# Expert rows gathered by quarters of channels and turned on VectorE in squares of 32, in an attention and mixture-of-experts kernel

## The chip, the cores and the metric

The kernel runs on one core of one Trainium2 chip. The metric is the device time of one execution in microseconds (us); three executions of the kernel before took 525.34, 525.06 and 520.8 us, median 525.06. The core has five engines with a queue each: TensorE (PE in the profile; its weight loads are PEld), VectorE (DVE), ScalarE (ACT), GpSimd (POOL) and SyncE (SP). [...]

## The reference

The first half is attention with a window and a few global keys; its output, 3072 tokens by 512 channels, is `x`. The second half sends each token to the one expert with the highest cosine score:

```python
logits = xn @ en.T / tau
expert_idx = np.argmax(logits, axis=1)
...
gate_w = probs[np.arange(N), expert_idx]
for e in range(E):                       # E = 8
    mask = expert_idx == e
    h = np.maximum(x[mask] @ w1[e], 0.0)               # 512 -> 1024
    out[mask] = gate_w[mask, None] * (h @ w2[e])       # 1024 -> 512
```

All is float32. The change lies in the second half alone.

## The kernel before, in words

**Attention** takes the first 200 us or so. It writes `x` to memory (`x_dram`, a row of 512 channels a token), chooses each token's expert, and scatters token number and gate into a list of slots by expert (`meta`). A first part of expert 0, 256 tokens, is already begun there.

**The loop over experts** (in the main function, from L1741) then runs eight stages; stage e computes expert e, up to 512 tokens. Each stage has an arm and, from expert 1 on, a pair. The arm (`tc.Switch`, L1384) is compiled for each width of tokens, in steps of 32, and one is chosen at run time; TensorE, ScalarE and VectorE enter it, GpSimd and SyncE don't. In the arm the product with w1 is done by `first_by_seven`: seven products of half-size blocks in place of eight (Strassen's method as Winograd has it), which needs sums of blocks of w1 (`fsum`, made by `first_sums`), and of the tokens (`xsum`, made by `token_sums`, which also overwrites a block of `xT`). Each product is 16 matmuls at L1312, and its result is added by VectorE at L1324 (`plus`); after a `plus` one list of `spare` work is done (`fill`). Behind it come the hidden sums (`hsum`, L1079 to L1082) and the product with w2 for tokens from 256 on (`second_in_arm`, L1245, and `part_in_arm`, L1258).

After the arm, the class `Pair` does the product with w2 for the first 256 tokens, again in seven products (L1117). `Pair.begin` runs the products m, n, n, n; VectorE adds u2 and u3 (L1122) and ScalarE scales them (u2g, u3g). `Pair.end` runs a product into the bank `ps`, which ScalarE reads and scales as p5 (L1170); then `fourth`; then a last product that adds into `ps`, and so has to wait for p5. The rest of the pair, one gated addition y (L1129), is done by VectorE in the next stage, right after its arm. `spare` lists of `Pair.begin` put sums between its additions.

The order on each engine is the order of the program (`manual_schedule`). So what stands ahead of an operation in its engine's queue delays it.

**The rows of the next expert.** `prepare(e + 1)` gathers the token rows with `gather_rows`: four indirect DMAs on GpSimd, each of 128 rows of 2 KB. GpSimd has nothing in the arm or the pair but these gathers and the scatters of results (L1264), so it works ahead: rows for expert e + 2 are gathered while TensorE is in stage e. The buffers `xg` hold eight tiles, two experts' rows. In stage e, `between` calls `turn_row` after some of the products: four TensorE transposes (L1026) of 128x128 into a bank, and two ScalarE copies (L1029) into `xT`, with the tokens laced: 16 by 16 into two halves.

Weights of experts 2 to 7 are loaded by `load_weights` on SyncE, w1 (L167) with channel c x 128 + p on partition p. The load of expert 2's waits for the last scatter of expert 0's results; later ones wait for the first product of the pair before (`out_again`). A `drain` on GpSimd (L1754) stands ahead of each stage.

Of the kernel before, what the change touches and what calls it, by code (L numbers as in the profile page):

```python
# [9 lines left out]
F32 = mybir.dt.float32  # L10
# [10 lines left out]
P = 128  # L21
# [2 lines left out]
PIECES = 32  # L24
FIRST = 256
LACE = 16
WIDTHS = [128] + list(range(160, CAP + 1, 32))
PAIR = WIDTHS.index(256)

# [134 lines left out]

def load_weights(k, e, w):
    nc = k.nc
    first = nc.sync.dma_start(w[0][:], k.w1[e].rearrange("(c p) f -> p c f", p=P))  # L167
    nc.sync.dma_start(w[1][:], k.w2[e].rearrange("(f p) m -> p f m", p=P))
    return first

# [824 lines left out]
def gather_rows(k, ids, xgp, NJ=CAP // P, upto=None):  # L995

    xgs, issued = [], []
    for j in range(NJ):
        xg = xgp.tile([P, k.DM], F32, name="xg", tag="xg")
        i = k.nc.gpsimd.indirect_dma_start(  # L1000
            out=xg[:], out_offset=None, in_=k.x_dram[0 : upto or k.N + 1, :],
            in_offset=bass.IndirectOffsetOnAxis(ap=ids[:, j, 0:1], axis=0),
        )
        xgs.append(xg)
        issued.append(i.ins)
    return xgs, issued


def new_turned(k):
    return k.xtp.tile([P, k.NC, 2, CAP // 2], F32, name="xT", tag="xT")  # L1010

# [280 lines left out]
            between(f)  # L1292


def first_by_seven(k, now, hT, w, between, spare):


    nc, h = k.nc, w // 2
    a = first_weights(k, now.w[0])
    b = [[now.xT[:, 2 * i : 2 * i + 2, j] for j in range(2)] for i in range(2)]  # L1300
    s1, s2, s3, s4 = now.first_sums
    t1, t2, t3, t4 = now.token_sums
    out = [[laced(hT[:, 4 * i : 4 * i + 4, 0:w])[:, j] for j in range(2)] for i in range(2)]
    number = [0]

    def banks():
        return [k.big.tile([P, CAP], F32, name="big", tag="big") for _ in range(2)]

    def product(to, x, y, add=False):
        for f in range(4):  # L1310
            for l in range(2):
                nc.tensor.matmul(to[f // 2][:, f % 2 * 256 : f % 2 * 256 + h], lhsT=x[:, l, f * P : (f + 1) * P], rhs=y[:, l, 0:h],  # L1312
                                 start=not (add or f % 2 or l), stop=True, skip_group_check=True)
        between(number[0])
        number[0] += 1

    def pairs(ps, q):
        for i in range(2):
            x = ps[i][:].rearrange("p (f n) -> p f n", f=2)[:, :, 0:h].rearrange("p f (q i) -> p f q i", i=LACE)
            yield x, q[:, 2 * i : 2 * i + 2]  # L1320

    def plus(ps, z, q, last=False):
        for (x, to), (_, z) in zip(pairs(ps, q), pairs(ps, z)):
            nc.vector.tensor_tensor(out=to, in0=x, in1=z, op=ALU.add)  # L1324
            if last:
                nc.scalar.activation(to, to, AF.Relu)  # L1326
        fill()

    def fill():
        for make in spare.pop(0):  # L1330
            make()

    (q11, q12), (q21, q22) = out
    fill()
    x, y = banks(), banks()
    product(x, a[0][0], b[0][0])
    for ps, q in pairs(x, q21):
        nc.scalar.copy(out=q, in_=ps)
    product(y, s2, t2)
    plus(y, q21, q12)  # L1340
    product(x, a[0][1], b[1][0], True)
    for ps, q in pairs(x, q11):
        nc.scalar.activation(q, ps, AF.Relu)
    product(y, s3, t3, True)
    plus(y, q21, q22)
    v = banks()
    product(v, s1, t1)
    plus(v, q22, q22, True)
    product(y, a[1][1], t4, True)
    plus(y, q21, q21, True)  # L1350
    product(v, s4, b[1][1], True)
    plus(v, q12, q12, True)


def expert(k, now, coming, widths, unfinished):


    tc = k.tc
    w1, w2 = now.w
    hT = new_hidden(k)  # L1360
    if coming:
        coming.xT = new_turned(k)

    def between(f):
        at = {1: (0,), 2: (1,), 3: (2,), 4: (3,)} if now.e else {5: (0,), 6: (1, 2), 7: (3,)}
        for j in at.get(f, ()) if coming else ():
            turn_row(k, coming.rows, coming.xT, j, k.nc.scalar.copy)

    a = [[hT[:, 4 * j : 4 * j + 4, i * P : (i + 1) * P] for j in range(2)] for i in range(2)]
    now.sums, spare = weight_sums(k, w2)  # L1370
    left, making = hidden_sums(k, a)
    more, ahead = [], []
    if coming:
        coming.token_sums, more = token_sums(k, coming.xT)
        if now.e:
            coming.first_sums, ahead = first_sums(k, coming.w[0])
    spare = [spare[:2], spare[2:], ahead[:1], ahead[1:2], more[:2], []]
    if now.e == 1:
        spare[2:6] = [], ahead[:1], ahead[1:2] + more[:1], more[1:2]
    tiles = range(2 if now.e else 1, CAP // P)  # L1380
    ps = None if now.e else k.work0.tile([P, k.DM], F32, name="work", tag="work")
    k.order = list(range(4, 8)) + list(range(4)) if now.e else list(range(8))
    steps = widths_of(now.e)
    for arm in tc.Switch(now.width.index, len(steps), hint=now.width.hint):  # L1384
        w = steps[arm]
        if now.e:
            first_by_seven(k, now, hT, w, between, list(spare))
            for make in making:
                make()
        else:  # L1390
            first_by_eight(k, now.xT, w1, hT, w, between)
        for size in (32, 64):
            if w % (2 * size) >= size:
                part_in_arm(k, now, hT, w2, w // (2 * size) * 2 * size, size)
        for j in tiles:
            if j < w // P:
                second_in_arm(k, now, hT, w2, j)
        if ps:
            second(k, ps, hT, w2, range(k.NF // 2))

    def scatters():
        for j in tiles:
            scatter_rows(k, now.y[:, j - 1, :], now.tile_ids[:, j : j + 1])
        for size in (64, 32):
            scatter_rows(k, now.y_part[size][:], now.parts[size][0], P // size)

    def choose_next():
        if coming:
            give_hint(k, coming.e, widths[coming.e])

    out = [scatters]
    if now.e:
        pair = Pair(k, now.rows, a, left, w2, now.sums, not coming)
        choose_next()
        out += unfinished.pop()()
        number = [lambda: widths.append(take_width(k, now.e + 2))] if now.e + 2 < k.E else []
        if now.e == k.E - 2:
            number.append(lambda: load_flag(k))
        if now.e == 2:
            ahead.append(lambda: flag_leftover(k))  # L1420
        pair.begin(spare=(more[2:], number + ahead[2:3], ahead[3:]))
        ps = k.work0.tile([P, k.DM], F32, name="work", tag="work")
        unfinished.append(pair.end(ps[:, 0:256]))
        out.append(pair.scatter(1))
    else:
        choose_next()
        widths.append(take_width(k, 2))
        out += unfinished.pop()()
        for make in more:
            make()  # L1430
        second(k, ps, hT, w2, range(k.NF // 2, k.NF))
        unfinished.append(lambda: end_second(k, now.rows, ps))
    return out
# [172 lines left out]
def kernel(  # L1606
# [40 lines left out]
    with ExitStack() as moe:  # L1647
# [43 lines left out]
        def prepare(e):  # L1691
            t = Net()
            t.e = e
            t.y, t.y_part = ys[e % 2]
            xgs, t.gathers = gather_rows(n, n.ids[:, e], n.xgp)
            t.rows = n.mt[:, e], n.ids[:, e], xgs
            if e < 2:
                t.w = n.w[e]
            else:
                t.w = new_weights(n, (wp_a, n.wp_b)[e % 2])  # L1700
            return t

        with tc.manual_schedule(engines=ORDERED | set(ARMS) | {mybir.EngineType.Pool}):
# [26 lines left out]
            for j in range(CAP // P):  # L1730
                turn_row(n, coming.rows, coming.xT, j, nc.vector.tensor_copy)
            cast(2, n.E)
            split_rows(n, n.mt)
            for y, parts in ys:
                for x in (y, *parts.values()):
# [5 lines left out]
            for e in range(n.E):  # L1741
                now, coming = coming, None
                parts_of(n, now)
                now.width = widths[e]
                if e == 1:
                    now.first_sums = first
                if e + 1 < n.E:
                    coming = prepare(e + 1)
                for scatter in pending:
                    scatter()  # L1750
                if e and coming:
                    wait_for(n, load_weights(n, e + 1, coming.w), [n.outs[-1] if e == 1 else n.out_again])

                nc.gpsimd.drain()  # L1754
                pending = expert(n, now, coming, widths, unfinished)
# [33 lines left out]
```

## Time and profile before

| | us |
|---|---|
| three executions | 525.34, 525.06, 520.8 |
| the profiled execution, its own time | 523.85 |
| its span in the profile | 522.0 |
| VectorE busy | 301.3 |
| ScalarE busy | 197.4 |
| GpSimd busy | 148.7 |

The stretches of the stages, and how busy TensorE and VectorE are in each, in us:

| stage | from | to | TensorE busy | VectorE busy | DMA share |
|---|---|---|---|---|---|
| 1 | 234.2 | 268.6 | 33.06 | 22.11 | 0.69 |
| 2 | 268.6 | 320.8 | 52.20 | 23.15 | 0.34 |
| 3 | 320.8 | 353.7 | 32.90 | 21.35 | 0.53 |
| 4 | 353.7 | 390.5 | 36.51 | 21.86 | 0.47 |
| 5 | 390.5 | 429.6 | 39.10 | 22.22 | 0.45 |
| 6 | 429.6 | 479.0 | 49.40 | 23.22 | 0.20 |
| 7 | 479.0 | 522.0 | 37.55 | 16.19 | 0.09 |

Stages differ with the number of tokens: 1 and 3 use the arm for 320, 4 for 352, 5 and 7 for 384, 6 for 480, 2 for 512. TensorE's granted clock was 0.994 over the span. In a row of the profile, a line such as L1312 is the line of the kernel that issued the instruction, the two names are output and input, and a releaser is what the engine had waited for. A busy share says little by itself; what counts is which work the chain of waits passes through in each stage.

### The profile page before, as it was taken

The page shows a single profiled execution, that of the slowest core. Times are in us where ns is not written, and L with a number is a line of the kernel's source. Part 1 is how long each engine was busy: PE and PEld are TensorE (multiplying, and loading weights), DVE is VectorE, ACT ScalarE, POOL GpSimd, SP SyncE. Part 2 cuts the span into 40 slices and gives each one's busy share as a digit, 9 for nine tenths or more (in the row PEclk, how much of TensorE's full clock was granted, in tenths as well). Part 3 has the DMA queues.
Part 4 walks back from the last instruction along what each step waited for, and adds up shares of the span by engine and source line. Part 5 has one row for each costly group of instructions (what it writes and reads, how often), then busy time and mean ns, then how long its engine had stood idle before and what let it go on. Part 6 is the DMA issues. An engine that isn't in the chain of part 4 may idle for free.

```text
span 522.0 us, 13698 instructions
## 1 busy us (share of the span) xinstructions
PE 500.9 (96%) x5606; PEld 412.8 (79%) x5606; DVE 301.3 (58%) x602; ACT 197.4 (38%) x493; POOL 148.7 (28%) x169
## 2 busy tenths in 40 slices
PE   8999999999987998899989999999999999999995
PEld 7777787787765687859878659989889789859964
DVE  5646667766774664846745606765646644715531
ACT  4966776777644311303222312412312222302210
POOL 4221121432443326253340024153053050013023
PEclk9999999999998999999999999999999999999999
DMA  8989999998524336818682018457066065001001
GB/s 166 202 174 182 220 238 217 222 232 204 131 69 121 104 62 143 251 46 290 207 287 99 2 50 285 156 198 263 3 217 242 4 224 164 1 15 68 0 22 67
DMA packets 111421, 76.32 MB, mean 146 GB/s; under 512 B 87077, under 2 KB 95269, under 8 KB 111281
## 3 DMA queue, kind: packets, MB, share of 16 engines
q1 hardware_dynamic: 102769, 59.00, 42.6%
q0 software_dynamic: 6912, 15.26, 8.7%
q8 instruction: 63, 1.03, 0.9%
q14 instruction: 77, 0.63, 0.5%
q10 hardware_dynamic: 1600, 0.39, 0.3%
HBM read 61.66 MB, written 17.16 MB: 151 GB/s over the span
## 4 chain that ended last, share of the span: by engine, by line
PE 64%; issue 24%; POOL 5%; DVE 3%; ACT 2%; POOLq 1%; DMA 1%; DVEq 0%
PE big L1312 15%; PE big L1117 8%; PE od L512 7%; PE pa L483 6%; PE pa L458 4%; PE work L1258 3%; PE od L522 3%; PE pa L681 3%; PE work L1117 3%; POOL out_dram L1264 3%; PE work L1245 3%; PE work L1026 2%; PE big L1288 2%; PE pa L585 2%; PE work L1036 1%
## 5 line engine op out<-in xcount | busy, mean ns | idle before, releaser
L496 DVE TENSOR_TENSOR ex<-ex,table 126x768 f32<-126x768 f32 x64 | 60.3, 947 | 41.4 <-ACT ex L489 38.5
L1324 DVE TENSOR_TENSOR hT<-big,hT 128x320 f32<-128x320 f32 (+4 forms) x70 | 39.4, 566 | 49.2 <-PE big L1312 46.8
L1264 POOL DMA_INDIRECT out_dram<-y_arm,tids x17 | 17.0, 1002 | 170.4 <-ACT y_arm L1247 121.3
L489 ACT ACTIVATE ex<-pa 126x384 f32<-126x384 f32 (+1 forms) x128 | 53.7, 476 | 24.0 <-PE pa L483 17.7
L1312 PE MATMUL big<-xT,w1t 128*128 128x160 f32 (+4 forms) x336 | 59.4, 330 | 1.3 <-issue 1.3
L1312 PEld LDWEIGHTS big<-xT,w1t 128*128 128x128 f32 x336 | 54.2, 190 | 4.0 <-issue 2.2
L512 PE MATMUL od<-ex,v 126*64 126x192 f32 (+1 forms) x576 | 46.8, 309 | 0.0
L1000 POOL DMA_INDIRECT xg<-x_dram,idss x32 | 32.3, 1011 | 43.9 <-PE big L1312 21.7
L483 PE MATMUL pa<-qT,kT 64*32 64x128 f32 (+3 forms) x2048 | 40.8, 268 | 2.8 <-issue 2.5
L483 PEld LDWEIGHTS pa<-qT,kT 64*32 64x32 f32 (+1 forms) x2048 | 30.5, 107 | 15.2 <-issue 10.6
L512 PEld LDWEIGHTS od<-ex,v 126*64 126x64 f32 x576 | 35.2, 138 | 7.7 <-issue 3.5
L259 POOL DMA_INDIRECT meta<-mt,slot x24 | 27.4, 1141 | 43.8 <-DVE rd L556 17.8
L1312 PE MATMUL big<-xsum,fsum 128*128 128x160 f32 (+4 forms) x224 | 39.6, 330 | 0.0
L1029 ACT COPY xT<-work 128x256 f32<-128x256 f32 x56 | 18.0, 377 | 56.7 <-PE work L1026 55.3
L1312 PEld LDWEIGHTS big<-xsum,fsum 128*128 128x128 f32 x224 | 36.1, 190 | 1.1
L1245 PE MATMUL work<-w2t,hT 128*128 128x512 f32 x80 | 35.1, 593 | 0.0
L1117 PE MATMUL big<-wsum,hsum 128*128 128x256 f32 x136 | 31.1, 380 | 1.5 <-issue 1.0
L1326 ACT ACTIVATE hT<-hT 128x320 f32<-128x320 f32 (+4 forms) x42 | 21.6, 533 | 25.5 <-DVE hT L1324 25.3
L433 POOL COPY v<-v 30x896 f32<-30x896 f32 (+1 forms) x15 | 16.6, 1119 | 49.0 <-DMA v<-in_v_dram 30.5
L1117 PEld LDWEIGHTS big<-wsum,hsum 128*128 128x128 f32 x136 | 25.7, 190 | 6.0 <-issue 1.8
L1245 PEld LDWEIGHTS work<-w2t,hT 128*128 128x128 f32 x80 | 15.1, 190 | 17.7 <-issue 17.6
L1122 DVE TENSOR_TENSOR ptmp<-big,ptmp 128x256 f32<-128x256 f32 x16 | 6.7, 421 | 37.6 <-PE big L1117 16.9
(246 smaller groups left out, 903.0 us busy)
## 6 DMA issues: line engine op xcount, KB each, us to landing
w1t<-in_moe_w_dram SPq DMA_DIRECT2D x6, 2048.0 KB
w2t<-in_moe_w_dram SPq DMA_DIRECT2D x6, 2048.0 KB
v<-in_v_dram SPq DMA_DIRECT2D x32, 192.0 KB
x_dram<-xs SPq DMA_DIRECT2D x23, 256.0 KB
k<-in_k_dram SPq DMA_DIRECT2D x28, 192.0 KB
q<-in_q_dram SPq DMA_DIRECT2D x28, 192.0 KB
w1t<-in_moe_w_dram SPq DMA_DIRECT2D x32, 128.0 KB
w2t<-in_moe_w_dram SPq DMA_DIRECT2D x32, 128.0 KB
```

The costliest lines, as they stand in the source:

```text
L259: i = nc.gpsimd.indirect_dma_start(out=k.meta[:], out_offset=bass.IndirectOffsetOnAxis(ap=slot[:, t : t + 1], axis=0), in_=mt[:, t, :], in ...
L483: i = nc.tensor.matmul(u.sp[e][k0:k1, a * n + c0 : a * n + c1], lhsT=t.kT[rows, j, k0:k1], rhs=t.qT[rows, j * BLK + c0 : j * BLK + c1], st ...
L489: nc.scalar.activation(u.ex[:, e], u.sp[e][0:ROWS, 0 : 2 * u.n].rearrange("p (a c) -> p a c", a=2), AF.Exp, scale=k.scale)
L496: nc.vector.tensor_tensor(out=exv, in0=exv, in1=tab[:, :, 0 : u.n // BLK, :], op=ALU.mult)
L512: nc.tensor.matmul(g.od[a][e * D : (e + 1) * D, at : at + c1 - c0], lhsT=g.v[0:ROWS, 2 * a + e, u.j, :], rhs=u.ex[:, e, a, c0:c1], start=f ...
L1000: i = k.nc.gpsimd.indirect_dma_start(out=xg[:], out_offset=None, in_=k.x_dram[0 : upto or k.N + 1, :], in_offset=bass.IndirectOffsetOnAxis ...
L1117: i = self.k.nc.tensor.matmul(ps, lhsT=x[:, f, :], rhs=w[:, f, :], start=f == 0 and not add, stop=True, skip_group_check=True)
L1245: nc.tensor.matmul(ps[:], lhsT=hT[:, f, j * P : (j + 1) * P], rhs=w2[:, f, :], start=i == 0, stop=i == k.NF - 1)
L1264: i = k.nc.gpsimd.indirect_dma_start(out=k.out.rearrange("t (i m) -> (t i) m", i=n), out_offset=bass.IndirectOffsetOnAxis(ap=ids, axis=0), ...
L1312: nc.tensor.matmul(to[f // 2][:, f % 2 * 256 : f % 2 * 256 + h], lhsT=x[:, l, f * P : (f + 1) * P], rhs=y[:, l, 0:h], start=not (add or f ...
L1324: nc.vector.tensor_tensor(out=to, in0=x, in1=z, op=ALU.add)
L1326: nc.scalar.activation(to, to, AF.Relu)
```

## The change

For experts 2 to 7, rows are no longer turned by TensorE.

- `square_rows` makes a list of row numbers once: `x_dram` is seen as 4 rows of 128 channels a token, and each gather takes, for 32 tokens, their four quarters of channels onto the four groups of 32 partitions.
- `gather_quarters` issues 16 gathers of 128 quarter rows (512 B) an expert, in place of 4 of whole rows. For expert 2, ten stand ahead of the scatters of expert 0's results and six behind them.
- `turn_squares` turns one tile of 128 tokens with one VectorE transpose of 32x32 squares from `xg` straight to `xT`, reading every fourth word. Partition p of `xT` then holds channels 4p to 4p + 3.
- `load_weights` loads w1 of experts 2 to 7 to match: four neighbouring rows a partition.
- The turns stand after the arm, behind the rest of the former pair and ahead of the pair's first addition. All four token sums come after that first addition; two of them stood in the arm before. In the arm, the sums of w2 (`wsum`) move from ahead of the first addition to behind it, and the sums of w1 (`fsum`) to the last two places; the third and fourth sum of w1 both come at the end of `Pair.begin`.

Experts 0 and 1 keep their gathers and their transposes.

```diff
 def load_weights(k, e, w):
-    first = nc.sync.dma_start(w[0][:], k.w1[e].rearrange("(c p) f -> p c f", p=P))
+    first = nc.sync.dma_start(w[0][:], k.w1[e].rearrange("(p c) f -> p c f", p=P))
...
+def square_rows(k):
+    k.squares = k.tp.tile([P, k.E, CAP // P, 4], I32, name="squares")
+    for b in range(4):
+        for g in range(4):
+            k.nc.vector.tensor_scalar(out=k.squares[b * SQ : (b + 1) * SQ, 2:, :, g], in0=k.mt[g * SQ : (g + 1) * SQ, 2:, :, 0],
+                                      scalar1=4.0, scalar2=float(b), op0=ALU.mult, op1=ALU.add)
+
+def gather_quarters(k, ids, xgs, lo, hi):
+    src = k.x_dram[:, :].rearrange("t (b c) -> (t b) c", b=4)
+    for i in range(lo, hi):
+        j, g = divmod(i, 4)
+        k.nc.gpsimd.indirect_dma_start(
+            out=xgs[j][:, g * P : (g + 1) * P], out_offset=None, in_=src,
+            in_offset=bass.IndirectOffsetOnAxis(ap=ids[:, j, g : g + 1], axis=0),
+        )
+
+def turn_squares(k, xgs, xT, j):
+    half = P // 2
+    k.nc.vector.transpose(
+        out=xT[:, :, :, j * half : (j + 1) * half].rearrange("p c a (g i) -> p g c a i", i=LACE),
+        in_=xgs[j][:].rearrange("p (g r c) -> p g c r", g=4, r=SQ),
+    )
...
 def expert(k, now, coming, widths, unfinished):
     def between(f):
-        at = {1: (0,), 2: (1,), 3: (2,), 4: (3,)} if now.e else {5: (0,), 6: (1, 2), 7: (3,)}
-        for j in at.get(f, ()) if coming else ():
+        for j in {5: (0,), 6: (1, 2), 7: (3,)}.get(f, ()):
             turn_row(k, coming.rows, coming.xT, j, k.nc.scalar.copy)
...
+            turns = [lambda j=j: turn_squares(k, coming.rows[2], coming.xT, j) for j in range(CAP // P)]
-    spare = [spare[:2], spare[2:], ahead[:1], ahead[1:2], more[:2], []]
-    if now.e == 1:
-        spare[2:6] = [], ahead[:1], ahead[1:2] + more[:1], more[1:2]
+    spare = [[], spare[:2], spare[2:3], spare[3:], ahead[:1], ahead[1:2]]
...
-            first_by_seven(k, now, hT, w, between, list(spare))
+            first_by_seven(k, now, hT, w, list(spare))
...
-        pair.begin(spare=(more[2:], number + ahead[2:3], ahead[3:]))
+        for make in turns:
+            make()
+        pair.begin(spare=(more, number, ahead[2:]))
...
-            xgs, t.gathers = gather_rows(n, n.ids[:, e], n.xgp)
+            if e < 2:
+                xgs, t.gathers = gather_rows(n, n.ids[:, e], n.xgp)
+            else:
+                xgs = [n.xgp.tile([P, n.DM], F32, name="xg", tag="xg") for _ in range(CAP // P)]
+                gather_quarters(n, n.squares[:, e], xgs, 0, 10 if e == 2 else 16)
...
             cast(2, n.E)
+            square_rows(n)
...
                 for scatter in pending:
                     scatter()
+                if e == 1:
+                    gather_quarters(n, n.squares[:, 2], coming.rows[2], 10, 16)
                 if e and coming:
                     wait_for(n, load_weights(n, e + 1, coming.w), [n.outs[-1] if e == 1 else n.out_again])
```

In `first_by_seven` the calls of `between` after each product are gone with it.

More of the change, by code (lines that the diff above doesn't have):

```diff
@@ L26 @@
 LACE = 16
+SQ = 32
 WIDTHS = [128] + list(range(160, CAP + 1, 32))
@@ L1292, in first_by_eight, with first_by_seven @@
             between(f)
-def first_by_seven(k, now, hT, w, between, spare):
+def first_by_seven(k, now, hT, w, spare):
     nc, h = k.nc, w // 2
@@ L1303, in first_by_seven @@
     out = [[laced(hT[:, 4 * i : 4 * i + 4, 0:w])[:, j] for j in range(2)] for i in range(2)]
-    number = [0]
     def banks():
@@ L1313, in product @@
                                  start=not (add or f % 2 or l), stop=True, skip_group_check=True)
-        between(number[0])
-        number[0] += 1
     def pairs(ps, q):
@@ L1371, in expert @@
     left, making = hidden_sums(k, a)
-    more, ahead = [], []
+    more, ahead, turns = [], [], []
     if coming:
```

## The prediction

> **What bounds the kernel now.** I read the page's busy table, then the chain of waits between 318 and 356 us (expert 3's stage), VectorE's timeline in the same stretch, and GpSimd's and SyncE's timelines around 215 to 245 us. "Stage e" is the work of expert e in the loop.
>
> ```profile
> PE 500.9 (96%) x5606; PEld 412.8 (79%) x5606; DVE 301.3 (58%) x602; ACT 197.4 (38%) x493; POOL 148.7 (28%) x169
> ```
>
> TensorE is busy 96% of the span. In stage 3 the chain is TensorE alone (start, length, line, count):
>
> ```profile
> 320.97 4.35 PE big L1312 x32
> 325.32 0.44 PE work L1026 x4
> 325.76 2.18 PE big L1312 x16
> ...
> 333.59 4.35 PE big L1312 x32
> 337.94 3.60 PE work L1258 x32
> 341.55 7.10 PE big L1117 x32
> 348.65 1.73 PE work L1117 x8
> 350.38 1.73 PE big L1117 x8
> 352.10 1.73 PE work L1117 x8
> ```
>
> Seven products of 2.18 us (L1312), four groups of transposes (L1026) between them, the arm's part (L1258), then seven products of 1.73 us of the pair. Nothing waits: time taken off TensorE here is time off the end, unless something else becomes late. What could is VectorE, which has this between the arm and the pair's third product:
>
> ```profile
> 341.06 0.69 DVE L1082 TENSOR_TENSOR hsum<-hT,hsum 128x512 f32<-128x512 f32 x1
> 344.39 0.48 DVE L1129 SCALAR_TENSOR_TENSOR y<-work,mts,u2g 128x256 f32<-128x256 f32 x1 [2.64 <-DMA out_dram<-y_arm,tids]
> 345.31 0.42 DVE L1122 TENSOR_TENSOR ptmp<-big,ptmp 128x256 f32<-128x256 f32 x1 [0.43 <-PE big L1117]
> 345.65 0.68 DVE L1056 TENSOR_TENSOR xsum<-xT 128x512 f32<-128x512 f32 x1
> 346.36 0.69 DVE L1057 TENSOR_TENSOR xsum<-xT,xsum 128x512 f32<-128x512 f32 x1
> 346.97 0.42 DVE L1122 TENSOR_TENSOR ptmp<-big,ptmp 128x256 f32<-128x256 f32 x1
> ```
>
> Only 0.43 us idle ahead of the first addition (u2, L1122 at 345.31), and 2.64 us in which VectorE leaves the arm. The new turns go between the y and u2.
>
> [...] the trace agrees (273 ns at L1026), but pipelined, four cost 0.44 us. [...] The turn reads every fourth word. [...] the reduction at L577 reads every eighth word,
>
> ```profile
> L577 DVE TENSOR_REDUCE lg<-lh x8: 500/504/509, 49.4 to 179.6; 128x24 f32<-128x192 f32 x8
> L1057 DVE TENSOR_TENSOR xsum<-xT,xsum x7: 691/692/693, 233.5 to 471.7; 128x512 f32<-128x512 f32 x7
> L1057 DVE TENSOR_TENSOR wsum<-w2t,wsum x8: 1224/1225/1225, 189.9 to 486.2; 128x1024 f32<-128x1024 f32 x8
> ```
>
> The two L1057 rows give 1.04 ns an element and 159 ns fixed; with that, L577 pays (504-159)/192 = 1.80 ns. [...] the gathers beside such sums at 238 to 243 us took 0.95 to 1.44 us, so a little at most.
>
> **The change, part by part.**
>
> 1. *Transposes leave TensorE.* Rows of experts 2 to 7 are turned in stages 1 to 6: 6 x 4 groups x 0.4385 us = **10.5 us off**. Stage 0 keeps its own, as do the rows of expert 0. The 48 ScalarE copies (377 ns) were never awaited by TensorE: nothing. Can the arm's VectorE keep the closer pace of 2.18 us? Two halves of an addition start 1.09 us apart, the second is followed at 0.41 by a sum of 1.13: the next half starts 0.45 late, and the half after it on time. Yes, even at the narrowest width, 320.
>
> 2. *Turns on VectorE*, four a stage. As a two-input sum of its size, one would take 0.61 us from start to start; at L577's rate 159 + 512 x 1.80 = 1.08 us, 1.00 from start to start, as the L1079 ops overlap by 0.08; [...] I take **t = 1.0**, [...] and keep 2.2 (twice my value) open, since no row shows a transpose. What waits behind them: u2, then all four token sums (L1054 to L1057), u3, ScalarE's u3g and p5 in order; and TensorE's seventh product adds into the bank that p5 reads. From the end E of the arm's last L1312 product (337.94 in stage 3): the last addition's half starts at +0.04; a w1 sum that now stands behind it ends the wait at +1.57 (hidden sums began at +1.07 before); hidden sums end at +4.31; arm left at +6.95; y, 0.41; turns 4t from +7.36; u2 0.34; four token sums 2.76; u3 0.42; u3g and p5 (0.51, 0.47) end at **+11.85 + 4t**. The seventh product starts at 352.10 = +14.16. So TensorE waits 4t - 2.3.
>  - Stage 3: 4.0 - 2.3 = **1.7 us**.
>  - Stage 1: the y is L1044's (0.75, so +0.2): 4t - 2.1 = **1.9**.
>  - Stage 4: the seventh product is at 388.89, E at 372.30, so 4t - 4.7: none[...]. Stage 5: 4t - 5.5, none. Stages 2 and 6 have a 128-token tile more in the arm and over 7 us to spare.
>  The waits of each turn for four gathers, 50 ns each in VectorE's queue, lie under the op before: nothing, at most 0.6 a stage.
>
> 3. *Sums moved.* Weight sums go from ahead of the first addition to behind it (2 x 1.14 us in a gap of 4.3 us), fsum's last two behind the last gated addition: they end near +17.3 at t = 1, and the next stage's second product starts at about +20. Nothing; late by 3 us they would cost what they are late.
>
> 4. *Sixteen gathers an expert for four on GpSimd.* Each costs 0.95 + 0.30 us between; rows of 512 B shouldn't cost more, as scatters of 512 B and 1 KB rows (L1264, 979 to 982 ns) equal those of 2 KB (1000). So 12 x 1.26 = 15.1 us more a stage, on an engine that waits 12 to 39 us for the arm. They come a whole stage ahead of the turn: about 4 us after the last scatter plus 20 us, in a stage of 31 us or more; rows land ahead of need. Scatters slip a few us; no buffer waits for them.
>
> 5. *Stage 1's tight spot.* Ten of expert 2's gathers stand ahead of expert 0's scatters, and w1 of expert 2 waits for the last of these:
>
> ```profile
> 219.55 0.95 POOL L1000 DMA_INDIRECT xg<-x_dram,idss  x1 [0.30 <-issue]
> 223.97 1.03 POOL L1264 DMA_INDIRECT out_dram<-y_arm,tids  x1 [3.47 <-issue]
> 233.19 1.15 POOL L1264 DMA_INDIRECT out_dram<-y,ids  x1 [0.30 <-issue]
> 236.94 0.38 SPq L167 DMA_DIRECT2D w1t<-in_moe_w_dram  x1
> ```
>
>  Ten from 215.79 end at 228.0; five scatters at 1.3 and two at 1.48 put the last at 236.35, 3.2 later. So w1 is issued at 240.1. Before, its first sum ran at 246.97 without waiting; now it would be due at 247.9, and with 10 us from issue to use at most it finds w1 between 248 and 250. I take 249: 1.1 late, of which 0.2 is caught up: **0.9 us** (0 to 2). The six gathers behind the scatters end near 245.5 and land by 250; the turn is at 257. [...] in later stages w1 has some 25 us to spare.
>
> 6. *Square rows*: 16 small VectorE ops at 0.16 (as L1230) = 2.7 us near 210 to 213, covered by 5.8 us of idleness ahead of 229.22 and done before the gathers start at 215.79. Without cover, 2.7.
>
> **Sum**, against the profiled execution (span 522.0, its own time 523.85): -10.5 + 1.7 + 1.9 + 0.9 = **-6.0**, to 517.85. The median shown, 525.06, is 1.2 above that execution: **519.0 us**. A difference under 1% (5 us) can't be told from no change here.
>
> **Rivals.**
> - *B, the turn streams at full rate* (t = 0.61). [...] against: L577. Stage 3 waits 0.1, stage 1 1.2: -9.2, **515.9**.
> - *C, VectorE becomes the bound.* The turns stand between the arm and u2, so TensorE waits at the pair's seventh product in stages 1, 3, 4 and 5: (4t - 1.2) + (4t - 2.3) + (4t - 4.7) + (4t - 5.5) = 16t - 13.7. It eats the gain from **t = 1.5** on. At t = 2.2: 21.5 - 10.5 = +11, **536**. For it: 4-byte squares with a strided read are shown nowhere; against: 1.8 ns at L577.
> - *D, the gathers are dearer.* At 1.67 us each, expert 2's last land when wanted, and w1 is 4 us later: -6.0 + 4.1, **523.2**. Against: the even price of the scatters.
> - That the change doesn't do what it says, leaving transposes in the arms, the code excludes; if TensorE had been waiting under cover of them, idle would show at L1312, and doesn't (1.3 us in 336).
>
> **The numbers.** Mine 0.45 (own range 516.5 to 522; 0.30 of it past 1%), B 0.25 (faster), C 0.20 (0.15 slower, 0.05 within), D 0.10 (0.06 within, 0.04 slower). Faster 0.55, same 0.26, slower 0.19. The range goes from all gain and no wait (514) to t of about 1.9 (530).
>
> **What would show it.** L1026 down to 32 transposes; the turn's mean (1.0 to 1.1 us right, over 1.5 wrong); a gap on TensorE ahead of the pair's seventh product in stages 1 and 3 of 1 to 3 us and none in 2 and 6; the first w1 sum of stage 1 waiting on the DMA; gathers still 0.95 us. A wait for gathers at the turns, or gaps at L1312, would make the prediction wrong.

## The result and the profile after

The changed kernel took **562.59 us** (median of four: 557.87, 562.17, 563.0, 573.56), the kernel before beside it 524.13: a ratio of 1.0715, interval 1.0622 to 1.0807. It is slower, where 519.0 and "faster" had been forecast. Times are medians of all executions; ratios and intervals leave out those that ran some per cent longer at a lower granted clock, so a ratio needn't be the quotient of two medians. The profiled execution took 563.0 us, its span is 561.3, TensorE's granted clock 0.960 (0.994 before).

The groups of instructions of the profile after (columns as before) show the change doing what it says:

```profile
L1024 POOL DMA_INDIRECT xg<-x_dram,squares x96 | 104.9, 1092 | 59.3 <-issue 44.4 <-PE big L1341 7.1 <-PE work L1056 6.9
L1033 DVE STREAM_TRANSPOSE xT<-xg 128x512 f32<-128x512 f32 x24 | 24.3, 1067 | 0.0
L1056 PE MATMUL work<-ident,xg 128*128 128x128 f32 x32 | 4.3, 273 | 1.1 <-DMA xg<-x_dram,idss 1.1
```

The transposes on TensorE are down from 128 to 32 (L1026 before is L1056 now), the 24 turns (L1033) wait for nothing, and the 96 quarter gathers (L1024) are there. The loss is somewhere else. The chain of waits of the profile after, from stage 0 to the start of stage 2 (start, length, engine, tile, line, count):

```profile
216.95 0.78 PE work L1288 x20
217.74 0.38 PE work L1288 x3
218.12 1.03 issue
219.15 0.31 PE work L1288 x2
219.47 1.11 issue
...
226.70 1.04 issue
227.74 1.95 PE work L1288 x29
...
265.01 4.00 DVE xT L1033 x4
269.01 6.83 another core or an unknown queue
...
279.13 7.24 another core or an unknown queue
...
287.79 3.78 PE work L1147 x8
```

The 64 matmuls of the arm's part (L1258 before, L1288 now) wait for nothing new between them. Before, they took 4.1 us, with two short stops (TensorE's timeline: start, length, line, tiles, shape, count, idle before and its releaser):

```profile
218.42 1.07 PE L1258 MATMUL work<-w2t,hT 128*32 128x128 f32 x29
220.04 0.47 PE L1258 MATMUL work<-w2t,hT 128*32 128x128 f32 x5 [0.56 <-issue]
221.50 1.12 PE L1258 MATMUL work<-w2t,hT 128*32 128x128 f32 x30 [0.99 <-issue]
```

After the change, 23 run at full pace, then one to three at a time, and between them TensorE stands for 1.0 to 1.1 us in "issue": it waits for nothing that the profile shows. The 64 take 12.8 us. In stage 1 the turns end at 269.0, and then VectorE stands for 6.83 and 7.24 us and TensorE's seventh product starts at 287.79. Stages 0, 1, 3, 4 and 5 hold such gaps. GpSimd was issuing its gathers or the scatters behind them in nearly all of them (ten gathers from 213.5 to 226.1; sixteen from 257.4 to 277.8 and five scatters to 284.5). Stages 6 and 7, which have no gathers, have none; neither has stage 2, in spite of its sixteen.

A first reading is that these engines lack instructions. The DMA view of the stretch 217.1 to 227.1 us (queue and kind: packets, MB, share of 16 engines) has

```profile
q0 software_dynamic: 248, 0.52, 17.9%
q14 instruction: 1, 0.01, 0.3%
```

The page has q8 and q14 as queues of the kind "instruction": 64 packets with 1.05 MB and 78 with 0.64 MB in the execution, so blocks of 16 and 8 KB. In these 10 us came one block of 8 KB and none of 16. The next of 16 KB came between 227.1 and 229, a microsecond after the tenth gather's end, and the matmuls ran at full pace from 227.74. But it began only at about 227.5 and took 1.1 us (3.7% of 16 engines over 1.9 us), so they set off before it was there. From 265.4 to 288.2 us there was again only one block, at 265.5; VectorE's two stops ended, at 275.9 and 286.4, without a new one. Whether these blocks are what the engines stand for is taken up with the second trace of the changed kernel below. The DMA engines themselves were idle most of the 10 us from 217.1 to 227.1 (q0, the gathers, took 17.9% of them, q14 0.3%).

In the stretches that hold gaps the granted clock is lower too (before, it was 1.00 from 198 to 240 us), and the eight matmuls right behind the gaps of stage 0 (L1066) took 5.57 us; in i1_after, told below, they took 3.70. The stretches of stages 0 and 1 (stretch, length, busy times and counts of PE, PEld, DVE, ACT, POOL, then granted clock, DMA share, GB/s):

```profile
206.20:241.90 35.70, 28.31 (x176) 20.72 (x177) 20.41 (x61) 5.38 (x17) 17.33 (x18) 0.86 0.34 104
241.90:291.40 49.50, 34.96 (x202) 29.30 (x201) 25.21 (x36) 7.01 (x16) 28.07 (x29) 0.83 0.48 172
```

Stage lengths from the start of one stage's first product to the next, in us; the forecast is that of the prediction's own terms; the last column is the changed kernel again in i1_after:

| stage | before | forecast | after | i1_after |
|---|---|---|---|---|
| 1 | 34.4 | 35.4 | 49.4 | 35.4 |
| 2 | 52.2 | 50.4 | 50.4 | 51.1 |
| 3 | 32.9 | 32.8 | 36.5 | 33.3 |
| 4 | 36.8 | 35.0 | 47.5 | 34.5 |
| 5 | 39.1 | 37.4 | 44.7 | 37.4 |
| 6 | 49.4 | 47.6 | 47.6 | 47.6 |

With stage 0 (35.7 for 26.4) these are 40.6 us more than before; the spans differ by 39.3.

### The profile page after: what moved, and what is told of

Its sections match the earlier page's. It is cut to its first block, busy times and chain, and to the rows that moved or that the text cites. A ratio compares the mean times of both kernels' runs of the same rounds, so it can differ in the third digit from the quotient of the medians.

```text
span 561.3 us, 13592 instructions
## 1 busy us (share of the span) xinstructions
PE 506.5 (90%) x5510; PEld 409.2 (73%) x5510; DVE 325.4 (58%) x642; ACT 183.8 (33%) x445; POOL 227.8 (41%) x241
## 3 DMA queue, kind: packets, MB, share of 16 engines
q8 instruction: 64, 1.05, 0.9%
## 4 chain that ended last, share of the span: by engine, by line
PE 65%; issue 18%; POOL 4%; DVE 4%; another core or an unknown queue 3%; ACT 2%; DMA 2%; POOLq 1%; ACTq 0%; DVEq 0%
PE big L1341 17%; PE od L513 7%; PE big L1147 7%; PE pa L484 6%; PE work L1275 4%; PE work L1147 4%; PE pa L459 4%; PE work L1288 3%; PE od L523 3%; PE pa L682 2%; POOL out_dram L1294 2%; PE pa L586 2%; PE big L1318 2%; PE work L1066 2%
## 5 line engine op out<-in xcount | busy, mean ns | idle before, releaser
L1024 POOL DMA_INDIRECT xg<-x_dram,squares x96 | 104.9, 1092 | 59.3 <-issue 44.4
L497 DVE TENSOR_TENSOR ex<-ex,table 126x768 f32<-126x768 f32 x64 | 60.2, 946 | 42.2 <-ACT ex L490 39.1
L1341 PEld LDWEIGHTS big<-xT,w1t 128*128 128x128 f32 x336 | 56.1, 194 | 4.6 <-ACT hT L1365 1.8
L1275 PE MATMUL work<-w2t,hT 128*128 128x512 f32 x80 | 37.1, 616 | 4.5 <-issue 4.5
L1288 PE MATMUL work<-w2t,hT 128*32 128x128 f32 (+1 forms) x320 | 29.0, 356 | 12.2 <-issue 12.1
L434 POOL COPY v<-v 30x896 f32<-30x896 f32 (+1 forms) x15 | 18.4, 1239 | 49.4 <-DMA v<-in_v_dram 16.7
L1341 PEld LDWEIGHTS big<-xsum,fsum 128*128 128x128 f32 x224 | 36.5, 190 | 1.7 <-ACT y L1194 0.4
L1288 PEld LDWEIGHTS work<-w2t,hT 128*32 128x32 f32 (+1 forms) x320 | 17.4, 134 | 22.5 <-issue 18.2
L1147 PE MATMUL big<-w2t,hT 128*128 128x256 f32 x112 | 29.2, 390 | 4.7 <-issue 3.1
L1275 PEld LDWEIGHTS work<-w2t,hT 128*128 128x128 f32 x80 | 15.4, 198 | 23.8 <-issue 23.6
L1147 PE MATMUL big<-wsum,hsum 128*128 128x256 f32 x136 | 31.1, 380 | 0.5 <-ACT ptmp L1173 0.5
```

The lines of the kernel that those rows point to most:

```text
L497: nc.vector.tensor_tensor(out=exv, in0=exv, in1=tab[:, :, 0 : u.n // BLK, :], op=ALU.mult)
L1024: k.nc.gpsimd.indirect_dma_start(out=xgs[j][:, g * P : (g + 1) * P], out_offset=None, in_=src, in_offset=bass.IndirectOffsetOnAxis(ap=ids[ ...
L1147: i = self.k.nc.tensor.matmul(ps, lhsT=x[:, f, :], rhs=w[:, f, :], start=f == 0 and not add, stop=True, skip_group_check=True)
L1275: nc.tensor.matmul(ps[:], lhsT=hT[:, f, j * P : (j + 1) * P], rhs=w2[:, f, :], start=i == 0, stop=i == k.NF - 1)
L1288: nc.tensor.matmul(ps[i * size : (i + 1) * size, 0:m], lhsT=hT[:, f, base : base + size], rhs=w2[:, f, i * m : (i + 1) * m], start=o == 0, ...
```

## The experiments

Theory G, a conjecture of the author's: GpSimd's gathers, one behind the other, keep new instructions from the other engines. It has two parts: that the gathers make the loss, which the runs try, and how they do it, on which only the traces bear. Rivals: the turns and the new order on VectorE (T), the 16 KB runs of w1 (W), the way the arms' code falls on the blocks (L). The runs came in five groups (a "call" in the expectations), each on a chip of its own together with runs of the kernel before; that turned out to matter.

### First group: which part of the change

e1_before_quarters is the kernel before with only the gathers changed, e2_after_whole the changed kernel with only the gathers undone:

```diff
-                gather_quarters(n, n.squares[:, e], xgs, 0, 10 if e == 2 else 16)
+            xgs, t.gathers = gather_rows(n, n.ids[:, e], n.xgp)
```

> The kernel before, with nothing changed but the gathers of experts 2 to 7: sixteen of quarter rows in place of four of whole rows, in the order of the changed kernel (ten, the scatters, six, for expert 2). The rows land in other places, so the transposes work on rows in a different order; w1, turns and sums are as before. Theory G (the long unbroken run of GpSimd gathers keeps new instructions from the other engines): about 565 us, the 53 us lost in the changed kernel less what depends on where its code lies, so 550 to 580, with gaps on TensorE that the profile ascribes to nothing while gathers run. Rival T (the turns on VectorE and the new order of its work make the loss): 524, as before. Rival W (the 16 KB runs of w1): 524. Rival L (the shorter code of the arms falls badly on the blocks in which instructions are fetched): 524.

> The changed kernel with the four whole-row gathers an expert of the kernel before; turns, w1 and sums stay as changed. Rows then lie a token on a partition, so the turned squares are not the right ones. G: the gaps go and the predicted gain of the other parts shows, 515 to 521. T, W or L: about 562, as changed.

Measured: e1 **588.99 us**, ratio 1.1161 (1.1039 to 1.1282); e2 **517.79 us**, 0.9897 (0.9816 to 0.9978). The gathers alone make the kernel before slower, by more than the 550 to 580 us expected; without them the rest of the change gains 1.0%, against 1.3% forecast for it (10.5 - 1.7 - 1.9 us, as w1 isn't late here). T, W and L fall as the cause of the loss.

e3_after_w1 undoes the load of w1 (`(c p) f`), e4_after_strips keeps sixteen gathers of a quarter of the rows:

```diff
-            out=xgs[j][:, g * P : (g + 1) * P], out_offset=None, in_=src,
-            in_offset=bass.IndirectOffsetOnAxis(ap=ids[:, j, g : g + 1], axis=0),
+            out=xgs[j][g * SQ : (g + 1) * SQ, :], out_offset=None, in_=k.x_dram[0 : k.N + 1, :],
+            in_offset=bass.IndirectOffsetOnAxis(ap=ids[0:SQ, j, 0:1], axis=0),
```

> The changed kernel with w1 of experts 2 to 7 loaded as before (channel c x 128 + p on partition p, 2048 rows of 4 KB), so channels of tokens and weights do not match. G, T and L: 562, within 1%. W: falls by the share that the 16 KB runs cost, towards 520 to 540.

> The changed kernel with sixteen gathers an expert of 32 whole rows each (the same first 32 tokens of a tile to each of the four groups of partitions) in place of 128 quarter rows: as many DMA instructions, as many bytes, a quarter of the rows. G with the number of instructions deciding: as changed, 550 to 565. G with the rows, or the time of a gather, deciding: if a gather's duration on GpSimd falls with its rows, 520 to 535. T and L: 562 either way.

Measured: e3 573.11 us, 1.1002 (1.0902 to 1.1102): the loss is there without W, so W is out; whether the 16 KB runs gain anything can't be told, as the changed kernel itself has no run on this chip. e4 585.22 us, 1.1165 (1.1059 to 1.1271). Both lie above what was expected (562 within 1%, and 550 to 565): the loss is larger on this chip. With a quarter of the rows, a gather still took 974 ns (1067 with 128 rows in e3), and the loss is not smaller than e3's (1.1165 against 1.1002): with the same 96 gathers, fewer rows did not make it smaller.

### Second group: how many, and what else would do

f2_filler (first line below, added to e2) has four whole-row gathers behind sixteen GpSimd operations; f3_eight (the next three) has ten gathers; f5_gaps (the last two) has all sixteen with pauses of two such operations (powers of a 128x3 tile, 987 ns each there):

```diff
+                fill_pool(n, 16)
...
+                gather_quarters(n, n.squares[:, e], xgs, 0, 8)
+                for j in (2, 3):
+                    n.nc.gpsimd.indirect_dma_start(out=xgs[j][:], out_offset=None, in_=n.x_dram[0 : n.N + 1, :],
...
+        if i % 4 == 0 and i > 0:
+            fill_pool(k, 2)
```

f4_sync gathers four times and moves blocks with SyncE, between w1 and w2:

```diff
+    for b in range(4):
+        for g in range(4):
+            k.nc.sync.dma_start(xq[b * SQ : (b + 1) * SQ, :, g * P : (g + 1) * P], xr[g * SQ : (g + 1) * SQ, :, b * P : (b + 1) * P])
```

> The changed kernel with four whole-row gathers an expert (as in the second run), and ahead of them sixteen small GpSimd operations (powers of a 128x3 tile, 1.05 us each) for each of experts 2 to 7: GpSimd is busy as long as with sixteen gathers, but issues no more DMAs than before; the turned squares are again not the right ones. If it is the indirect DMAs that keep instructions away: 515 to 521, as the second run's 517.8. If any long busy stretch of GpSimd does it: 550 or more.

> The changed kernel with ten gathers an expert: two tiles by quarters of channels (eight gathers), two tiles by whole rows (two gathers, whose turned squares are not the right ones); all stand ahead of the scatters for expert 2 too. If each gather beyond four costs its share: (10 - 4)/(16 - 4) of the 45 us between the second run and the changed kernel, 22 on top of 518, so 535 to 545. If only long unbroken runs do harm: under 525.

> The changed kernel with four whole-row gathers an expert, whose blocks are then put into squares by sixteen plain DMAs on SyncE from SBUF to SBUF (128 pieces of 512 B each), between the loads of w1 and w2; for expert 2 ahead of both. Whole computation. If only GpSimd's indirect DMAs do harm: the second run's time and little more, 516 to 521, so faster than before by 0.5 to 1.3%. If any run of many small DMAs does: 550 or more.

> The changed kernel with two of the small GpSimd operations of the first run of this call (2.4 us) between every four gathers: as many gathers, but never more than four in a run; whole computation. If a pause lets a block of instructions through (fetches of 16 KB took about 1.1 us): 525 to 548. If the count decides and pauses do not help: 560 or more.

Measured: f2 523.14 us, 1.0092 (1.0067 to 1.0118); f3 513.83, 0.9912 (0.9886 to 0.9938); f4 **513.54**, 0.9900 (0.9882 to 0.9918); f5 519.75, 1.0016 (0.9998 to 1.0034). f4 came as G expects; f2 lies 2 us above its 515 to 521, f5 5 us below its 525 to 548, both within 1% of the kernel before. But f3 lost nothing at all, with seventeen DMAs of GpSimd in a row in stage 0, the first eight just those of the changed kernel: what comes later in the queue can't have stopped the changed kernel at its fourth gather. So the chip came under suspicion (rival H), and the changed kernel was run beside the others.

### Third group: with the changed kernel as a control

> The changed kernel once more, as a control, since the last call ran on another chip than the first and its kernel with ten gathers lost nothing although its first eight gathers stand as in the changed kernel. If the number and spacing of gathers make the loss (theory G): 558 to 574, as at first. If the loss hangs on the chip, or on where a kernel's instructions lie (rival H): near the kernel with pauses, 512 to 525.

> The kernel with pauses between every four gathers, again, beside the changed kernel on one chip. G: 516 to 530 while the changed kernel takes 558 to 574. H: about as the changed kernel, plus 0 to 8 us for the small operations: where that takes 560, this takes 560 too.

> The kernel with four gathers an expert and squares made by SyncE's plain DMAs, again, on the same chip. G: 512 to 520. H: where the changed kernel takes 560, this too, 540 or more.

> The kernel with ten gathers an expert (eight of quarters, two of whole rows), again, on the same chip. G by share: 530 to 545 on a chip where the changed kernel takes 560. G with a threshold: 512 to 520 there. H: as the changed kernel.

Measured on one chip: changed 555.14 us, 1.0658 (1.0591 to 1.0724); pauses 527.1, 1.0069 (1.0039 to 1.0099); SyncE's squares **514.65**, 0.9877 (0.9846 to 0.9909); ten gathers 531.1, 1.0234 (1.0156 to 1.0313). On a chip that loses, the loss goes with the number of gathers (ten: 16 us above the SyncE kernel, which has four; sixteen: 40), and pauses take two thirds of it away. In the kernel with pauses GpSimd does more than in the changed kernel (in f5 the same 96 gathers, and 36 small operations of 35.5 us in all), so its busy time alone is not what costs here. f3 and this run of ten gathers are one kernel: 0.9912 there, 1.0234 here.

### Fourth and fifth group: chips without the loss

> The changed kernel as a control on this chip: 545 to 575 where the loss is as on the two chips before, 512 to 525 if this chip shows none, in which case the three others tell nothing.

> Four whole-row gathers an expert behind sixteen small GpSimd operations (the turned squares are not the right ones), again. If the DMAs do it: 515 to 526 while the changed kernel takes 545 or more. If GpSimd being busy does it: 545 or more too.

> The changed kernel in which the fifth, ninth and thirteenth gather of an expert each wait until the one before has landed, about 2 us without a DMA being issued, and nothing else is added; whole computation. If pauses let instructions through: 514 to 528, a little under the kernel with pauses made of operations (527). If it was the operations, or only the slower pace: 540 or more.

> The same with one such wait, ahead of the ninth gather: runs of eight. If the number of gathers in a run decides: as the kernel with ten gathers an expert (531), so 525 to 545. If one pause were enough: 514 to 524.

> The changed kernel on one chip more. From the calls so far either 545 to 575 ([...] as on the chips where the kernel before took 521 to 524) or 512 to 518 (as on the last one, where the kernel before took 518.7); nothing between is expected.

> Runs of eight gathers, with one wait for a landing between. On a chip where the changed kernel takes 545 or more: 525 to 545 if the number of gathers in a run decides, under 525 if one pause is enough, 545 or more if such a pause does not help. On a chip without the loss: 515 to 520, as in the last call, which tells nothing new.

h0 and i1 are the changed kernel, h1 is f2 again. In h2 the gather before must have landed ahead of every fourth, in h3 and i2 of every eighth:

```diff
+        if i > lo and i % 4 == 0:
+            wait_for(k, this, [last])
```

Measured: h0, the changed kernel, **514.99 us**, 0.9931 (0.9907 to 0.9955); i1, the same on a fifth chip, **514.33 us**, 0.9875 (0.9824 to 0.9926). Nothing is lost here. h1 521.89, 1.0063 (1.0046 to 1.0080); h2 531.65, 1.0240 (1.0209 to 1.0271); h3 517.32, 0.9972 (0.9951 to 0.9993); i2 518.95, 0.9994 (0.9971 to 1.0017). So on these chips pauses only cost: the four are 2.3 to 16.7 us above the changed kernel beside them. In h2 VectorE's waits show for what (line, releaser: total, times, longest):

```profile
DVE fsum L1112 <- DMA w1t<-in_moe_w_dram: 8.8, 1, 8.8
DVE xT L1036 <- DMA xg<-x_dram,squares: 6.8, 1, 6.8
```

w1 of expert 2 comes late behind the scatters, and a turn waits for its gathers: GpSimd's time was not as free as it looked. Whether landings help on a chip that loses isn't known. The filler kernel, too, has run only where nothing is lost.

The two traces of the changed kernel can be laid side by side. In i1 the DMA view of 217.1 to 227.2 us, with eight gathers being issued, has

```profile
q0 software_dynamic: 256, 0.52, 17.9%
...
q14 instruction: 4, 0.03, 1.4%
q8 instruction: 2, 0.03, 1.3%
```

and TensorE's timeline (start, length, line, tiles, shape, count, idle before and its releaser)

```profile
218.96 1.95 PE L1288 MATMUL work<-w2t,hT 128*32 128x128 f32 x64
...
249.85 1.95 PE L1288 MATMUL work<-w2t,hT 128*64 128x256 f32 x16 [0.96 <-ACT hT L1353]
253.28 1.97 PE L1147 MATMUL big<-w2t,hT 128*128 128x256 f32 x8 [1.49 <-DVE hsum L1111]
...
265.16 1.99 PE L1147 MATMUL work<-w2t,hsum 128*128 128x256 f32 x8 [1.28 <-ACT ptmp L1200]
...
349.51 1.99 PE L1147 MATMUL work<-w2t,hsum 128*128 128x256 f32 x8 [1.81 <-ACT ptmp L1200]
```

The same gathers at nearly the same pace, about as many packets of q0, but six instruction blocks in place of one, and the 64 matmuls in 1.95 us in place of 12.8.

Counted by place in the program, and not by time, the blocks don't differ. The instruction queues from 0 to 220.5 us in i1 and from 0 to 227.4 us in the first trace, then TensorE of i1 from 218.96 to 220.5 us:

```profile
q8 instruction: 31, 0.51, 1.1%
q14 instruction: 12, 0.10, 0.3%
...
q8 instruction: 31, 0.51, 1.1%
q14 instruction: 12, 0.10, 0.2%
...
218.96 1.74 PE L1288 MATMUL work<-w2t,hT 128*32 128x128 f32 x56
```

With 31 blocks of 16 KB and 12 of 8 KB, i1 had started 56 of the 64 matmuls without a stop; with the same 31 and 12 the first trace had run 35, and stood again and again. So in this stretch TensorE had no need of the blocks that were missing, and that so few came in 10 us may follow from the stops as well as cause them. The first reading isn't shown, and here the traces speak against it.

## Why the prediction was wrong, and where it was right

1. **Transposes leave TensorE, -10.5: right.** Stages 2 and 6, which had nothing else, became 1.8 us shorter in the trace after, as forecast (4 x 0.4385 = 1.75); in i1 it was 1.1 and 1.8.
2. **Turns, t = 1.0, then a wait of 4t - 2.3: right.** A turn took 1.07 us, four 4.0. In i1 the seventh product waited 1.81 us in stage 3 (1.7 forecast) and 1.28 in stage 1 (1.9; TensorE came late there itself), and not in 4 and 5. In the first trace the gaps cover this. Rivals B and C, which lived from t, fall.
3. **Sums moved: nothing, right.** No group shows a wait behind them.
4. **Sixteen gathers for four: this is the step that failed.** "So 12 x 1.26 = 15.1 us more a stage, on an engine that waits 12 to 39 us for the arm" counted what the gathers cost GpSimd, and that was near enough (1.09 us each in place of 0.95). It named a cover for GpSimd's own time and for the landing of the rows, and put the gathers' effect on the other engines at nothing without a reason. On the chips of the result and of the first and third group these engines stand while gathers are issued; in the trace after, TensorE stood 12.1 us at L1288 and 4.5 at L1275 for nothing that the profile shows, and 10.7 at L1147 for ScalarE. On the first group's chip, with the gathers undone in e2, the loss is gone; with them alone in e1, it is all there. D, the rival on gathers, looked at their duration only and was wrong the same way. The prediction's own sign of being wrong, "gaps at L1312", was seen, at other lines, but no case of the forecast held it. The profile of before already had a little of it: the part at L1258 in stage 0, shown above, took 4.1 us beside its four gathers, and 1.95 in i1. The prediction left stage 0 out, as it was not to change.
5. **w1 of expert 2 late: mechanism right, size off.** In i1 VectorE's first sum of w1 waited 2.30 us for the DMA and TensorE stood 0.96 + 1.49 = 2.45 us, against 0.9.
6. **Square rows covered: right.** Sixteen in 3.1 us; TensorE has no wait for them.

The sum, with step 4 at nothing, was -6.0 us. On the chips that lose nothing the change brought -3.7 (514.99 for 518.69, by the interval 2.3 to 4.8 less) and -4.5 (514.33 for 518.8). With step 5 at its measured size the sum is -4.5, which lies within both intervals; -6.0 lies outside the first. e2 brought -5.6 (517.79 for 523.39). So the working held but for the size of step 5 and for step 4, which was worth 40 us on the chip of the third group (555.14 with sixteen gathers against 514.65 with four) and 55 on that of the first (e3 573.11 against e2 517.79).

**A version that keeps the gain on a chip that loses** is f4_sync (again as g3_sync_again): 0.9877 of the time before on a chip on which the changed kernel loses, and 0.9900 on one where that was not run, at 514.65 and 513.54 us. Where the changed kernel loses nothing (0.9931 and 0.9875), no run shows it to be better.

**Open:** how a run of gathers stops the other engines, and why it does so on the chips of the result and of the first and third group, and not on those of the fourth and fifth, nor for the sixteen beside stage 2. A gather took as long on both (1092 ns in the first trace, 1098 in i1), and the DMA engines were mostly idle (18.2% busy from 217.1 to 227.1 us in the first trace), so neither of these accounts for it. That it is the chip, and not something else that differs from group to group, is argued from few chips, not shown. The kernel before, with its four gathers, took 521.3 to 524.1 us where the changed kernel or e1 lost, and 518.7 to 519.1 in the other groups, so it may lose a little there itself.

## What to carry to other kernels

An engine with spare time was not a free place for more DMA instructions here: its own time was covered, and yet, on the chip of the first group, the kernel before took 523.39 us with four gathers an expert and 588.99 with sixteen. Where TensorE stands in "issue", see what the other engines do in each such gap, and change that alone, both ways, as e1 and e2 do. Before something that is missing during a stop is called its cause, count it by place in the program in a run that doesn't stop: here one instruction block came in 10 us where six came in i1, yet the run that stood had the same 31 and 12 by then. And put the kernel under test beside its variants on every chip: a variant that looks cured may only have met another chip, as the ten gathers may have (0.9912 in one group, 1.0234 in another).

## What was not expected of the hardware

- Beside a run of ten gathers of 128 rows (one each 1.25 to 1.6 us), 64 matmuls that waited for nothing the profile shows took 12.8 us on one chip and 1.95 on another, with the same instruction blocks there (31 of 16 KB and 12 of 8 KB).
- A gather of 32 rows cost GpSimd 974 ns, one of 128 rows 1067 ns (e4 and e3, on one chip): a quarter of the rows took off 93 ns.
- A 128x512 VectorE transpose in 32x32 squares, read at every fourth word, took 1.07 us, close to the 1.08 worked out from a reduction that read every eighth.
